# First block's low parts on VectorE alone, weight loads queued ahead of waiting loads, and the places of the last projection's operands

## The chip, the cores and the metric

The kernel runs on one core of a Trainium2 chip. The metric is device microseconds from start to end of one execution. TensorE (PE) does matmuls and PEld its weight loads, VectorE is DVE, ScalarE is ACT, GpSimd is POOL, and SyncE (SP) only issues DMAs.

## The reference

36 tiles of 128 tokens go through three stages, all in float32:

```
attention in chunks of 64:  attn = softmax(q k^T / 8),  out = attn v
first MLP (512 -> 2048 -> 512):   h = x w_in;  g = h * clip(h + 3, 0, 6) / 6;  x' = g w_out
second MLP (512 -> 1024 -> 512):  h = x' w_in2;  s = h * softmax(h);  y = layernorm(s) * g_ln;  out = y w_out2
```

## The kernel before, in words

**Stages.** Tokens are worked in 9 blocks of 512 (b), each of 4 attention units (u) of 128 tokens. While block b goes through the first MLP, the attention of block b+1 is done in between; block 0's four units are done ahead of it (here "the head"). After the ninth block the second MLP runs over 36 tiles of 128 tokens: h2 (L482, 24 matmuls), softmax, layernorm, and the projection out_t (L564, 24 matmuls) three tiles later.

**Two-part operands.** A float32 operand is cut into a high part (a cast by ScalarE into float32r, L73) and a low part (a subtraction, L74), and each product is three matmuls: high·high, high·low, low·high. So x, g, every weight and the normalised tile l have a `_hi` and a `_lo`; `split` makes both, and its last argument says which engine subtracts.

**One step of the first MLP.** For each of 16 slices f of the hidden width, TensorE does 12 matmuls into `hp` (H(f), L272), ScalarE a relu (L278), VectorE the gate (L282), then g is split, and 12 matmuls add into `acc` (O(f), L298). The program order on TensorE is H(f), O(f-1), H(f+1), O(f), so that H(f+1) covers the work on g(f). `hp`, t, g_hi and g_lo have two buffers each. Every fourth step carries an attention unit: `slot` puts in its scores and its product with v (f = 3, 7, 11, 15), exp and norm (f = 0, 4, 8, 12) and transposes (f = 2, 6, 10, 14).

**Weights in block 0.** The inputs' weights arrive as 64-bit words and are turned into float32 in the first block only: `fetch` loads them (SP), `rescale` (L142, ScalarE) scales the high word, `convert` (VectorE) makes the sign (L152) and two word steps (L157), and `split_w` makes the two parts, the low one on GpSimd. In step f the weights wo f and wi f+3 are converted, and g_lo, too, is made by GpSimd in this block. From block 1 on the weights stand in SBUF and VectorE makes g_lo.

**Order.** Each engine runs its instructions strictly in the order in which the code is written. SP too: a load that waits for a buffer holds all loads behind it.

**Places.** Where a tile lies in a partition is fixed when the program is built. In bytes modulo 512, all tiles that the large matmuls read lie at 192 (x_hi, x_lo, wi, wo, g_hi, g_lo) except l_hi and l_lo of the last projection: they stand in pool b3, behind b2's small [P, 1] tiles, at 0 (the first l_hi at byte 173056, while the wi it meets are at 66240 + 4096 f).

Of the kernel before, what the change touches and what calls it, by code (L numbers as in the profile page):

```python
# [8 lines left out]
F32 = mybir.dt.float32  # L9
F32R = mybir.dt.float32r  # L10
# [11 lines left out]
def tile_kernel(  # L22
# [76 lines left out]
    pbd = ap1.tile([P, 2, H, D], F32, name="pbd")  # L99
    q_t, k_t, v_t, p_t, exps, sums, raws, ready = {}, {}, {}, {}, {}, {}, {}, []  # L100

    def att_tile(pool, tag):
        return pool.tile([P, H, D], F32, tag=tag, name=tag)
# [39 lines left out]

    def convert(*keys):

        work = []
# [4 lines left out]
        for key, r, s in work:  # L151
            nc.vector.tensor_single_scalar(  # L152
                out=s, in_=r[:, :, 1], scalar=-(1 << 31), op=ALU.bitwise_and
            )
        for w, op, shift in ((0, ALU.logical_shift_right, 29), (1, ALU.logical_shift_left, 3)):
            for key, r, s in work:
                nc.vector.scalar_tensor_tensor(  # L157
                    out=s, in0=r[:, :, w], scalar=shift, in1=s, op0=op, op1=ALU.bitwise_or
                )
        for (kind, f), r, s in work:  # L160
            w = s.bitcast(F32)
            if kind == "2" and f >= KD * NS:
                nc.vector.tensor_scalar_mul(
                    out=w, in0=w, scalar1=g_sb[:, f - KD * NS : f - KD * NS + 1]
                )
            t = SLOTS[kind](f, F32R)
            (wo if kind == "o" else wi)[f] = t
            ready.append((t[:, 0], t[:, 1], w))

    def split_w(n=2):  # L170
        while ready and n:
            split(*ready.pop(0), nc.gpsimd)
            n -= 1

    def att_psum():
# [32 lines left out]

    def attn_exp_act(u):
        sc, mx = exps.pop(u)  # L210
        p_t[u] = att_tile(ap2, "p")
        sums[u] = ap2.tile([P, H], F32, tag="sm", name="sm")
        for h in range(H):
# [41 lines left out]

    def attn_pv(u, pb, x_hi, x_lo, ps=att_psum):
# [8 lines left out]
        split(x_hi[:, :, o : o + P], x_lo[:, :, o : o + P], xps)  # L265

# [13 lines left out]

    def moe_g(hp, t, eng):
        nc.vector.scalar_tensor_tensor(  # L282
            out=t, in0=t, scalar=6.0, in1=hp, op0=ALU.min, op1=ALU.mult
        )
        g_hi = gp.tile([P, BT], F32R, tag="g_hi", name="g_hi")
        g_lo = gp.tile([P, BT], F32R, tag="g_lo", name="g_lo")
        split(g_hi, g_lo, t, eng)
        return g_hi, g_lo
# [25 lines left out]

    kbs, qps, vs = [kbd], [], []
    for i in range(3):
# [3 lines left out]
    vs = wo_slot(NF - 7, F32).rearrange("p c (h k) -> p c h k", h=H)  # L320

    load_qk(0)
    load_qk(1, qps[0][:, 0], diagonal(kbs[1], nc.gpsimd))
    load_qk(2, qps[1][:, 0], diagonal(kbs[2], nc.vector))
    fetch("i", 0)
    load_qk(3, qps[2][:, 0], diagonal(kbs[3], nc.gpsimd))
    load_v(0)
    load_v(1)
    fetch("i", 1)
    load_v(2, vs[:, 0])  # L330
    load_v(3, vs[:, 1])
    fetch("o", 0)
    fetch("i", 2)
    fetch("o", 1)
    nc.sync.dma_start(out=g_sb, in_=g_ln)
    make_identity(nc, ident)
    diagonal(pbd, nc.gpsimd)
    nc.gpsimd.memset(three, 3.0)
    xs = new_x()
    attn_scores(0)  # L340
    attn_scores(1)
    load_qk(4)
    attn_norm(0, nc.gpsimd)
    attn_scores(2, h_psum, qps[0][:, 1])
    attn_transpose(0, pbd, h_psum)
    rescale("i", 0)
    attn_norm(1)
    attn_scores(3, h_psum, qps[1][:, 1])
    attn_transpose(1, kbs[1])
    attn_norm(2)  # L350
    attn_pv(0, pbd, *xs)
    load_v(4)
    attn_transpose(2, kbs[2], h_psum)
    attn_norm(3)
    convert(("i", 0))
    attn_pv(1, kbs[1], *xs)
    load_v(5)
    rescale("i", 1)
    attn_transpose(3, kbs[3], h_psum)
    split_w(1)  # L360
    attn_pv(2, kbs[2], *xs)
    convert(("i", 1))
    attn_pv(3, kbs[3], *xs)
    rescale("i", 2)
    split_w(1)
    attn_scores_act(4)
    load_qk(5)
    for f in range(2, NF):
        if f < NF - 7:
            fetch("o", f)  # L370
        if f + 1 < NF:
            fetch("i", f + 1)
    for f in range(NF - 7, NF):
        fetch("o", f)
    convert(("i", 2))
    rescale("o", 0)
    rescale("i", 3)
# [25 lines left out]
    def slot(b, f):  # L403
        ph = (f + 1) % 4
        u = (b + 1) * UPB + (f + 1) // 4
        if ph == 0:
            w = u - 1
            if w < NU:
                attn_pv(w, pbd, *xn[w // UPB])
                p_t.pop(w, None)  # L410
                load_v(w + 2)
            start_scores(u)
        elif u < NU:
            first = u < 2 * UPB
            if ph == 1:
                if u in exps:
                    attn_exp_act(u)
                attn_norm(u)
            elif ph == 2 and not first:
                attn_transpose_dve(u, (0, 1))  # L420
            elif ph == 3:
                if first:
                    attn_transpose(u)
                else:
                    attn_transpose_dve(u, (2, 3))

    pend = []
    for b in range(NB):
        first, last = b == 0, b == NB - 1
        if not last:  # L430
            xn[b + 1] = new_x()
        for f in range(NF):
            h = moe_h(f, *xn[b])
            if first:
                split_w(1)
            pend.append((b, f, moe_g(*h, nc.gpsimd if first or last else nc.vector)))
            if f % 4 == 3:
                slot(b, f)
            if first:
                convert(("o", f), ("i", f + 3))  # L440
            if len(pend) > 1:
# [3 lines left out]
            if first:  # L445
                rescale("o", f + 1)
                rescale("i", f + 4)
            split_w(1 if first else 2)
            if last:
# [24 lines left out]
    def h2(t):  # L474
# [3 lines left out]
        for s in range(NS):  # L478
            n = 0
            for kk in range(KD):  # L480
                for a, w in ((x_hi, 0), (x_hi, 1), (x_lo, 0)):
# [12 lines left out]
        mu = b2.tile([P, 1], F32, tag="mu", name="mu")  # L494
        nc.vector.scalar_tensor_tensor(
# [150 lines left out]
```

## Time and profile before

| | |
|---|---|
| median of 3 runs | 1312.58 us (1311.85 to 1313.03) |
| the profiled execution | 1311.98 us, span 1310.0 us, mean granted TensorE clock 0.995 |
| busy share of the span: PE, DVE, ACT, POOL | 98%, 61%, 44%, 23% |
| matmuls | 6368 |
| waits of TensorE that the trace names | 28.5 us |
| moved by DMA | 92.41 MB |

The span runs from the first to the last instruction; some 2 us lie around it. The profile's page cuts the span into 40 slices of 32.75 us, and a digit there is a busy share in tenths. A timeline row is the start and duration in us, then engine, line, operation, out<-in, form and count, and in brackets the idle time ahead of it with what ended it. A chain row is a piece of the chain of work that ended last: start, duration, engine, output, line and the number of instructions merged.

### The profile page before, as it was taken

The numbers are of one execution on the slowest core, as the hardware profiler recorded it, in microseconds if no ns is written. First come the engines' busy times: TensorE is split into PE (matmuls) and PEld (weight loads), VectorE is DVE, ScalarE is ACT, GpSimd is POOL, SyncE is SP. The second block draws the span as 40 slices with busy tenths as digits, with TensorE's granted clock in tenths as the row PEclk, the third lists the DMA queues.
The fourth block names the chain that finished last, engine by engine and source line by source line (L and its number), as shares of the span: only waits on it lengthen the run. The fifth ranks groups of instructions, "written<-read, shape, count | busy, mean of one in ns | idle before, by whom it ended". The sixth has DMA issues, their size and how long they took to land.

```text
span 1310.0 us, 17877 instructions
## 1 busy us (share of the span) xinstructions
PE 1277.4 (98%) x6368; PEld 1041.7 (80%) x6368; DVE 794.0 (61%) x1556; ACT 581.8 (44%) x1106; POOL 298.5 (23%) x562
## 2 busy tenths in 40 slices
PE   6699999999999999999999999999999999999998
PEld 5566788888888888888888888888888888888887
DVE  6788655655655655656555555469766555555542
ACT  4566422222322222222322222445687666666665
POOL 2465200000000000000000000355355444444444
PEclk9899999999999999999999999999999999999999
DMA  7910110110110210200200200444132221222111
GB/s 236 409 62 25 57 49 25 57 49 25 58 47 25 77 29 25 81 25 25 81 25 28 78 25 1 129 129 129 28 94 82 80 81 49 81 81 73 57 49 57
DMA packets 52649, 92.41 MB, mean 71 GB/s; under 512 B 9552, under 2 KB 18768, under 8 KB 52560
## 3 DMA queue, kind: packets, MB, share of 16 engines
q1 hardware_dynamic: 52560, 91.27, 21.8%
q8 instruction: 50, 0.82, 0.2%
q14 instruction: 39, 0.32, 0.1%
HBM read 62.92 MB, written 18.87 MB: 62 GB/s over the span
## 4 chain that ended last, share of the span: by engine, by line
PE 89%; issue 3%; POOL 3%; DVE 2%; DMA 1%; ACT 1%; SPq 1%; POOLq 0%; ACTq 0%; DVEq 0%
PE acc L298 27%; PE hp L272 26%; PE po L564 15%; PE hp L482 15%; PE att L261 2%; PE att L186 2%; POOL g_lo L74 1%; POOL wo L74 1%; DMA wi<-in_moe_w_in 1%; DVE s L157 1%; POOL wi L74 1%; DVE s L152 1%; SPq L112 0%; DVE x_lo L74 0%; DVE t L282 0%
## 5 line engine op out<-in xcount | busy, mean ns | idle before, releaser
L298 PE MATMUL acc<-g_hi,wo 128*128 128x512 f32 x1152 | 295.0, 397 | 16.1 <-ACT wo L73 14.2
L272 PE MATMUL hp<-x_hi,wi 128*128 128x512 f32 x1152 | 285.1, 390 | 0.0
L298 PEld LDWEIGHTS acc<-g_hi,wo 128*128 128x128 f32 x1152 | 213.1, 189 | 73.1 <-ACT wo L73 18.9
L278 ACT ACTIVATE t<-hp,three 128x512 f32<-128x512 f32 x144 | 99.0, 687 | 372.6 <-PE hp L272 372.2
L272 PEld LDWEIGHTS hp<-x_hi,wi 128*128 128x128 f32 x1152 | 215.9, 188 | 44.9 <-ACT wi L142 0.2
L282 DVE SCALAR_TENSOR_TENSOR t<-t,hp 128x512 f32<-128x512 f32 x144 | 99.1, 688 | 234.4 <-ACT t L278 234.4
L74 POOL TENSOR_TENSOR g_lo<-t,g_hi 128x512 fp32r<-128x512 f32 x32 | 45.8, 1431 | 715.1 <-PE acc L298 672.5
L482 PE MATMUL hp<-wi,x_hi 128*128 128x512 f32 x576 | 177.8, 390 | 0.0
L298 PE MATMUL acc<-g_lo,wo 128*128 128x512 f32 x576 | 154.4, 390 | 0.0
L272 PE MATMUL hp<-x_lo,wi 128*128 128x512 f32 x576 | 153.9, 389 | 0.0
L564 PE MATMUL po<-wi,l_hi 128*128 128x512 f32 x576 | 140.2, 396 | 0.0
L251 DVE STREAM_TRANSPOSE pbd<-p 32x128 f32<-32x128 f32 x448 | 135.3, 302 | 5.7
L73 ACT CAST g_hi<-t 128x512 fp32r<-128x512 f32 x144 | 89.3, 620 | 107.9 <-DVE t L282 107.9
L564 PEld LDWEIGHTS po<-wi,l_hi 128*128 128x128 f32 x576 | 108.3, 188 | 25.6
L482 PEld LDWEIGHTS hp<-wi,x_hi 128*128 128x128 f32 x576 | 108.2, 188 | 23.5
L298 PEld LDWEIGHTS acc<-g_lo,wo 128*128 128x128 f32 x576 | 108.6, 189 | 22.9
L74 POOL TENSOR_TENSOR l_lo<-m,l_hi 128x1024 fp32r<-128x1024 f32 x36 | 86.6, 2406 | 174.1 <-ACT l_hi L73 152.0
L272 PEld LDWEIGHTS hp<-x_lo,wi 128*128 128x128 f32 x576 | 108.1, 188 | 22.5
L74 DVE TENSOR_TENSOR g_lo<-t,g_hi 128x512 fp32r<-128x512 f32 x112 | 77.6, 693 | 76.8 <-ACT g_hi L73 76.8
L516 ACT COPY m<-tr 32x256 f32<-32x256 f32 x288 | 115.8, 402 | 2.9
L482 PE MATMUL hp<-wi,x_lo 128*128 128x512 f32 x288 | 112.4, 390 | 0.0
L491 ACT ACTIVATE e<-hp,nmx 128x1024 f32<-128x1024 f32 x36 | 40.2, 1116 | 111.3 <-DVE nmx L488 111.3
(91 smaller groups left out, 1299.7 us busy)
## 6 DMA issues: line engine op xcount, KB each, us to landing
wi<-in_moe_w_in SPq DMA_DIRECT2D x24, 512.0 KB, 7.3
x2d<-xo SPq DMA_DIRECT2D x36, 256.0 KB, 2.8
xo<-x2d SPq DMA_DIRECT2D x36, 256.0 KB, 4.3
m<-tr SPq DMA_DIRECT2D x288, 32.0 KB, 1.8
out<-ob SPq DMA_DIRECT2D x36, 256.0 KB, 2.2
v<-in_v SPq DMA_DIRECT2D x34, 256.0 KB, 2.6
q<-in_q SPq DMA_DIRECT2D x33, 256.0 KB, 3.5
kbd<-in_k SPq DMA_DIRECT2D x66, 128.0 KB, 3.5
```

The costliest lines, as they stand in the source:

```text
L73: nc.scalar.copy(out=hi, in_=src)
L74: (eng or nc.vector).tensor_sub(out=lo, in0=src, in1=hi.bitcast(F32))
L186: nc.tensor.matmul(sc[r0 : r0 + D, h // 2], qt[:, h], kt[:, :, h], start=True, stop=True)
L251: nc.vector.transpose(out=pb[o : o + 32, s // 2, c, s % 2], in_=pv[s * 32 : s * 32 + 32, c, e],)
L272: nc.tensor.matmul(hp, wi[f][:, a, kk * P : (kk + 1) * P], b[:, kk], start=(n == 0), stop=(n == 3 * KD - 1),)
L278: nc.scalar.activation(out=t, in_=hp, func=AF.Relu, bias=three[:])
L282: nc.vector.scalar_tensor_tensor(out=t, in0=t, scalar=6.0, in1=hp, op0=ALU.min, op1=ALU.mult)
L298: nc.tensor.matmul(acc[dc], wo[f][:, w, dc * P : (dc + 1) * P], g[i], start=(f == 0 and n == 0), stop=(f == NF - 1 and n == 2),)
L482: nc.tensor.matmul(hp[:, s * DM : (s + 1) * DM], a[:, kk, o : o + P], wi[kk * NS + s][:, w], start=(n == 0), stop=(n == 3 * KD - 1),)
L491: nc.scalar.activation(out=e, in_=hp, func=AF.Exp, bias=nmx, accum_out=r)
L516: move(out=m[b * 32 : b * 32 + 32, a], in_=tr[a * 32 : a * 32 + 32, b])
L564: nc.tensor.matmul(po, a[:, f], wi[KD * NS + f][:, w], start=(n == 0), stop=(n == 3 * NF2 - 1),)
```

## The change

Low parts of g and of the weights are made by VectorE in block 0, in an order of three steps: in step f the signs of wo f+1 and wi f+3 stand between the gate and g_lo, the word steps behind the subtractions, and what they give is split in the next step (`split_w_hi`, `split_w_lo`, `moe_split` with `between`). An attention unit's exps are cut into two halves over two steps, with the norm moved to f = 1, 5, 9, 13. In the head the scores go to the four `acc` banks, the v products to `h`, the norm of unit 2 to GpSimd, the first weight's conversion stands ahead of norm 3, and low parts of x are put off. Weight loads are queued in ahead of q, k and v loads that wait for a buffer. In the second MLP the small tiles get a pool of their own (`bs`), and l_hi and l_lo three buffers with names of their own, which puts them at 192 modulo 512 (l_hi0 at byte 172736).

The core of the diff:

```diff
+    def split_w_hi(n=1):
         while ready and n:
-            split(*ready.pop(0), nc.gpsimd)
+            hi, lo, w = ready.pop(0)
+            nc.scalar.copy(out=hi, in_=w)
+            halves.append((hi, lo, w))
             n -= 1
+
+    def split_w_lo(eng):
+        for hi, lo, w in halves:
+            eng.tensor_sub(out=lo, in0=w, in1=hi.bitcast(F32))
+        halves.clear()
...
+    def moe_split(t, eng, between=None):
         g_hi = gp.tile([P, BT], F32R, tag="g_hi", name="g_hi")
         g_lo = gp.tile([P, BT], F32R, tag="g_lo", name="g_lo")
-        split(g_hi, g_lo, t, eng)
+        nc.scalar.copy(out=g_hi, in_=t)
+        if between:
+            between()
+        eng.tensor_sub(out=g_lo, in0=t, in1=g_hi.bitcast(F32))
         return g_hi, g_lo
...
     attn_transpose(1, kbs[1])
-    attn_norm(2)
-    attn_pv(0, pbd, *xs)
+    rescale("i", 0)
+    attn_norm(2, nc.gpsimd)
+    attn_pv(0, pbd, *xs, h_psum, lo=False)
     load_v(4)
-    attn_transpose(2, kbs[2], h_psum)
+    fetch("o", 2)
+    fetch("i", 4)
+    convert(("i", 0))
+    attn_transpose(2, kbs[2])
     attn_norm(3)
-    convert(("i", 0))
-    attn_pv(1, kbs[1], *xs)
+    attn_pv(1, kbs[1], *xs, h_psum, lo=False)
     load_v(5)
...
+    ahead = [[("o", f + 1), ("i", f + 3)] for f in range(NF)]
+    ahead[0].insert(0, ("i", 2))
...
-            h = moe_h(f, *xn[b])
+            hp, t = moe_h(f, *xn[b])
+            moe_gate(hp, t)
             if first:
-                split_w(1)
-            pend.append((b, f, moe_g(*h, nc.gpsimd if first or last else nc.vector)))
+
+                split_w(1, nc.vector)
+                g = moe_split(t, nc.vector, lambda: convert_signs(*ahead[f]))
+                split_w_hi(4)
+                split_w_lo(nc.vector)
+                convert_words()
+            else:
+                g = moe_split(t, nc.gpsimd if last else nc.vector)
+            pend.append((b, f, g))
             if f % 4 == 3:
                 slot(b, f)
-            if first:
-                convert(("o", f), ("i", f + 3))
             if len(pend) > 1:
                 moe_o(*pend.pop(0))
...
             if first:
-                rescale("o", f + 1)
+                rescale("o", f + 2)
                 rescale("i", f + 4)
-            split_w(1 if first else 2)
+            else:
+                split_w(2)
...
-    b3 = ctx.enter_context(tc.tile_pool(name="b3", bufs=3, reuse_waits="tile"))
+    b3 = ctx.enter_context(tc.tile_pool(name="b3", bufs=1, reuse_waits="tile"))
+    bs = ctx.enter_context(tc.tile_pool(name="bs", bufs=2, reuse_waits="tile"))
...
+    def l_tile(name, i):
+        return b3.tile([P, NF2, P], F32R, tag=f"{name}{i}", name=f"{name}{i}")
...
-        l_hi = b3.tile([P, NF2, P], F32R, tag="l_hi", name="l_hi")
-        l_lo = b3.tile([P, NF2, P], F32R, tag="l_lo", name="l_lo")
+        l_hi, l_lo = l_tile("l_hi", t % 3), l_tile("l_lo", t % 3)
```

**VectorE, step f = 3 of block 0.** Before, this is the gate of step 3 and what follows up to the next conversions (t is g's first form, s the word being built; wo3 and wi6 are the weights converted):

```order
L282 SCALAR_TENSOR_TENSOR t_568<-t_568,hp_555 128x512
L74 TENSOR_TENSOR x_lo_398<-att_577,x_hi_397 128x4x128
L205 TENSOR_REDUCE mx_599<-att_590 128x8
L206 TENSOR_SCALAR mx_599<-mx_599 128x8
L152 TENSOR_SCALAR s_606<-wo3_340 128x512
L152 TENSOR_SCALAR s_607<-wi6_350 128x512
L157 SCALAR_TENSOR_TENSOR s_606<-wo3_340,s_606 128x512
```

With the change, the same step:

```order
L311 SCALAR_TENSOR_TENSOR t_574<-t_574,hp_561 128x512
L186 TENSOR_TENSOR wo3_538<-s_527,wo3_538 128x512
L151 TENSOR_SCALAR s_582<-wo4_287 128x512
L151 TENSOR_SCALAR s_584<-wi6_289 128x512
L321 TENSOR_TENSOR g_lo_580<-t_574,g_hi_579 128x512
L186 TENSOR_TENSOR wi5_539<-s_529,wi5_539 128x512
L159 SCALAR_TENSOR_TENSOR s_582<-wo4_287,s_582 128x512
L159 SCALAR_TENSOR_TENSOR s_584<-wi6_289,s_584 128x512
L159 SCALAR_TENSOR_TENSOR s_582<-wo4_287,s_582 128x512
L159 SCALAR_TENSOR_TENSOR s_584<-wi6_289,s_584 128x512
L294 TENSOR_TENSOR x_lo_399<-att_595,x_hi_398 128x4x128
L223 TENSOR_REDUCE mx_617<-att_608 128x8
```

Three subtractions (wo3, g_lo, wi5) have come in, and wo is converted a step earlier than before.

**SP, the loads around q and k of unit 4** (q_177 and q_174 are those of unit 4, v_248 and v_278 or v_281 those of v 4 and 5). Before:

```order
L135 DMA wo1_137<-in_moe_w_out 128x1024
L335 DMA g_sb_60<-in_moe_g_ln 128x8
L110 DMA q_177<-in_q 128x512
L112 DMA kbd_93<-in_k 64x512 x2
L120 DMA v_248<-in_v 128x512
L120 DMA v_278<-in_v 128x512
L110 DMA q_332<-in_q 128x512
L112 DMA kbd_93<-in_k 64x512 x2
L135 DMA wo2_336<-in_moe_w_out 128x1024
L135 DMA wi3_338<-in_moe_w_in 128x1024
```

Now:

```order
L110 DMA q_174<-in_q 128x512
L112 DMA kbd_93<-in_k 64x512 x2
L135 DMA wo1_178<-in_moe_w_out 128x1024
L135 DMA wi3_180<-in_moe_w_in 128x1024
L120 DMA v_248<-in_v 128x512
L135 DMA wo2_250<-in_moe_w_out 128x1024
L135 DMA wi4_252<-in_moe_w_in 128x1024
L120 DMA v_281<-in_v 128x512
L135 DMA wo3_283<-in_moe_w_out 128x1024
```

wi3 stood behind the loads of v 4, v 5 and unit 5; now it stands ahead of all three, and wo2 to wi7 ahead of unit 5's.

**ScalarE, the end of the head** (the casts L285 make x_hi of units 1 to 3, L180 a weight's high part, L258 copies transposed probabilities; with the change):

```order
L285 CAST x_hi_144<-hp_271 128x4x128
L258 COPY wo13_99<-att_292 64x512 x2
L180 CAST wi0_258<-s_254 128x512
L142 ACTIVATE wi1_131<-wi1_131 128x512
L285 CAST x_hi_144<-hp_303 128x4x128
L142 ACTIVATE wo0_133<-wo0_133 128x512
L285 CAST x_hi_144<-hp_315 128x4x128
L180 CAST wi1_387<-s_383 128x512
L142 ACTIVATE wi2_135<-wi2_135 128x512
L142 ACTIVATE wo1_178<-wo1_178 128x512
L142 ACTIVATE wi3_180<-wi3_180 128x512
L307 ACTIVATE t_413<-hp_400,three_59 128x512
```

The rescales of wi1 and wo0 now stand ahead of the last two x_hi, and three rescales ahead of the first relu (L307).

## Rows read from the trace of the kernel before

**Rows 1.** The page: busy time by engine, 40 slices of TensorE, one group.

```profile
PE 1277.4 (98%) x6368; PEld 1041.7 (80%) x6368; DVE 794.0 (61%) x1556; ACT 581.8 (44%) x1106; POOL 298.5 (23%) x562
...
PE   6699999999999999999999999999999999999998
...
L74 DVE TENSOR_TENSOR g_lo<-t,g_hi 128x512 fp32r<-128x512 f32 x112 | 77.6, 693 | 76.8 <-ACT g_hi L73 76.8
```

**Rows 2.** Windows: width; busy us of PE, PEld, DVE, ACT, POOL; clock; DMA.

```profile
40.00:50.00 10.00, 6.88 (x21) 5.58 (x22) 9.93 (x15) 5.39 (x14) 4.83 (x4) 0.63 1.03 409
100.00:110.00 10.00, 8.07 (x32) 5.75 (x33) 9.21 (x14) 5.57 (x10) 6.49 (x5) 1.00 0.01 2
160.00:180.00 20.00, 20.00 (x112) 16.48 (x111) 10.94 (x25) 5.73 (x9) 0.00 (x0) 1.00 0.14 40
```

**Rows 3.** TensorE's waits: us in total, times, longest.

```profile
PE acc L298 <- ACT wo L73: 14.2, 7, 9.6
...
PE acc L298 <- POOL wo L74: 1.7, 10, 0.2
```

**Rows 4.** The chain in the first block.

```profile
81.99 1.47 POOL g_lo L74
...
110.49 1.47 POOL g_lo L74
...
138.97 0.44 PE att L236 x4
...
142.14 1.02 PE att L261 x16
143.17 0.87 PE att L186 x16
...
149.71 2.72 PE acc L298 x12
```

**Rows 5.** Timeline of VectorE and GpSimd in one stretch of block 0.

```profile
60.35 0.69 DVE L74 TENSOR_TENSOR x_lo<-att,x_hi 128x512 fp32r<-128x512 f32 x1 [1.17 <-ACT x_hi L73]
...
60.96 0.68 DVE L205 TENSOR_REDUCE mx<-att 128x8 f32<-128x512 f32 x1
...
61.76 0.43 DVE L152 TENSOR_SCALAR s<-wo 128x512 int32<-128x512 int32 x1
...
62.44 0.69 DVE L157 SCALAR_TENSOR_TENSOR s<-wo,s 128x512 int32<-128x512 int32 x1
...
64.24 0.69 DVE L157 SCALAR_TENSOR_TENSOR s<-wi,s 128x512 int32<-128x512 int32 x1
...
66.36 1.29 POOL L74 TENSOR_TENSOR wi<-s,wi 128x512 fp32r<-128x512 f32 x1
66.40 1.54 DVE L152 TENSOR_SCALAR s<-wo 128x512 int32<-128x512 int32 x1
...
71.70 0.16 DVE L226 TENSOR_SCALAR sm<-sm 128x8 f32<-128x8 f32 x1
...
72.14 1.67 DVE L228 TENSOR_TENSOR p<-p,sm 128x512 f32<-128x512 f32 x1
```

**Rows 6.** Timeline of the head and its end.

```profile
22.13 0.69 DVE L228 TENSOR_TENSOR wo<-wo,sm 128x512 f32<-128x512 f32 x1
...
23.19 1.42 DVE L157 SCALAR_TENSOR_TENSOR s<-wi,s 128x512 int32<-128x512 int32 x2
...
26.44 0.58 ACT L73 CAST x_hi<-att 128x512 fp32r<-128x512 f32 x1 [0.44 <-PE att L261]
...
27.81 2.11 PE L272 MATMUL hp<-x_hi,wi 128*128 128x512 f32 x8
...
35.80 0.65 ACT L142 ACTIVATE wi<-wi 128x512 f32<-128x512 f32 x1 [5.99 <-DMA wi<-in_moe_w_in]
```

**Rows 7.** The chain in the second MLP.

```profile
907.82 21.76 PE hp L482 x96
...
957.31 5.47 PE hp L482 x24
962.78 5.60 PE po L564 x24
...
1283.71 22.41 PE po L564 x96
```

More of the change, by code (lines that the diff above doesn't have):

```diff
@@ L99, in tile_kernel @@
     pbd = ap1.tile([P, 2, H, D], F32, name="pbd")
-    q_t, k_t, v_t, p_t, exps, sums, raws, ready = {}, {}, {}, {}, {}, {}, {}, []
+    q_t, k_t, v_t, p_t, exps, sums, raws = {}, {}, {}, {}, {}, {}, {}
     def att_tile(pool, tag):
@@ L142, in rescale, with convert_signs @@
             nc.scalar.activation(out=r, in_=r, func=AF.Copy, scale=2.0**-112)
-    def convert(*keys):
-        work = []
+    work, ready, halves = [], [], []
+    def convert_signs(*keys):
         for key in keys:
@@ L150, in convert, with convert_words @@
                 work.append((key, raws.pop(key).bitcast(I32), s))
[L151 to L154, printed above, removed]
+                nc.vector.tensor_single_scalar(
+                    out=s, in_=work[-1][1][:, :, 1], scalar=-(1 << 31), op=ALU.bitwise_and
+                )
+    def convert_words():
         for w, op, shift in ((0, ALU.logical_shift_right, 29), (1, ALU.logical_shift_left, 3)):
@@ L168, in convert, with split_w @@
             ready.append((t[:, 0], t[:, 1], w))
-    def split_w(n=2):
+        work.clear()
+    def convert(*keys):
+        convert_signs(*keys)
+        convert_words()
+    def split_w_hi(n=1):
         while ready and n:
-            split(*ready.pop(0), nc.gpsimd)
+            hi, lo, w = ready.pop(0)
+            nc.scalar.copy(out=hi, in_=w)
+            halves.append((hi, lo, w))
             n -= 1
+    def split_w_lo(eng):
+        for hi, lo, w in halves:
+            eng.tensor_sub(out=lo, in0=w, in1=hi.bitcast(F32))
+        halves.clear()
+    def split_w(n=2, eng=None):
+        split_w_hi(n)
+        split_w_lo(eng or nc.gpsimd)
     def att_psum():
@@ L207, in attn_scores_act, with attn_exp_act @@
         exps[u] = sc, mx
[L209 to L213, printed above, removed]
+    def attn_exp_act(u, heads):
+        sc, mx = exps[u]
+        if u not in sums:
+            p_t[u] = att_tile(ap2, "p")
+            sums[u] = ap2.tile([P, H], F32, tag="sm", name="sm")
+        for h in heads:
             nc.scalar.activation(
@@ L254, in attn_transpose_dve, with attn_pv @@
                     )
-    def attn_pv(u, pb, x_hi, x_lo, ps=att_psum):
+    def attn_pv(u, pb, x_hi, x_lo, ps=att_psum, lo=True):
         vt = v_t.pop(u)
@@ L264, in attn_pv, with attn_lo @@
         o = (u % UPB) * P
-        split(x_hi[:, :, o : o + P], x_lo[:, :, o : o + P], xps)
+        hi, lo_ = x_hi[:, :, o : o + P], x_lo[:, :, o : o + P]
+        nc.scalar.copy(out=hi, in_=xps)
+        los.append((lo_, xps, hi))
+        if lo:
+            attn_lo()
+    los = []
+    def attn_lo():
+        lo, xps, hi = los.pop(0)
+        nc.vector.tensor_sub(out=lo, in0=xps, in1=hi.bitcast(F32))
     def moe_h(f, x_hi, x_lo):
@@ L279, in moe_h, with moe_gate @@
         return hp, t
-    def moe_g(hp, t, eng):
+    def moe_gate(hp, t):
         nc.vector.scalar_tensor_tensor(
@@ L312, in moe_o @@
                 nc.sync.dma_start(out=x2d[b, :, dc], in_=xo)
-    kbs, qps, vs = [kbd], [], []
+    kbs, qps = [kbd], []
     for i in range(3):
@@ L320, in tile_kernel, with acc_psum, later @@
     vs = wo_slot(NF - 7, F32).rearrange("p c (h k) -> p c h k", h=H)
+    def acc_psum(i):
+        return lambda: ps_acc.tile([P, DM], F32, tag=f"acc{i}", name=f"acc{i}")
+    def later(f):
+        if f < NF:
+            fetch("i", f)
     load_qk(0)
@@ L324, in tile_kernel @@
     load_qk(2, qps[1][:, 0], diagonal(kbs[2], nc.vector))
-    fetch("i", 0)
     load_qk(3, qps[2][:, 0], diagonal(kbs[3], nc.gpsimd))
@@ L328, in tile_kernel @@
     load_v(1)
-    fetch("i", 1)
+    fetch("i", 0)
     load_v(2, vs[:, 0])
     load_v(3, vs[:, 1])
+    fetch("i", 1)
     fetch("o", 0)
     fetch("i", 2)
-    fetch("o", 1)
-    nc.sync.dma_start(out=g_sb, in_=g_ln)
     make_identity(nc, ident)
@@ L339, in tile_kernel @@
     xs = new_x()
-    attn_scores(0)
-    attn_scores(1)
+    attn_scores(0, acc_psum(0))
+    attn_scores(1, acc_psum(1))
     load_qk(4)
+    fetch("o", 1)
+    fetch("i", 3)
     attn_norm(0, nc.gpsimd)
-    attn_scores(2, h_psum, qps[0][:, 1])
-    attn_transpose(0, pbd, h_psum)
-    rescale("i", 0)
-    attn_norm(1)
-    attn_scores(3, h_psum, qps[1][:, 1])
-    attn_transpose(1, kbs[1])
-    attn_norm(2)
-    attn_pv(0, pbd, *xs)
+    attn_scores(2, acc_psum(2), qps[0][:, 1])
+    attn_transpose(0, pbd)
+    attn_norm(1)
+    attn_scores(3, acc_psum(3), qps[1][:, 1])
+    attn_transpose(1, kbs[1])
+    rescale("i", 0)
+    attn_norm(2, nc.gpsimd)
+    attn_pv(0, pbd, *xs, h_psum, lo=False)
     load_v(4)
-    attn_transpose(2, kbs[2], h_psum)
+    fetch("o", 2)
+    fetch("i", 4)
+    convert(("i", 0))
+    attn_transpose(2, kbs[2])
     attn_norm(3)
-    convert(("i", 0))
-    attn_pv(1, kbs[1], *xs)
+    attn_pv(1, kbs[1], *xs, h_psum, lo=False)
     load_v(5)
-    rescale("i", 1)
-    attn_transpose(3, kbs[3], h_psum)
-    split_w(1)
-    attn_pv(2, kbs[2], *xs)
+    fetch("o", 3)
+    fetch("i", 5)
+    fetch("o", 4)
+    fetch("i", 6)
+    attn_lo()
+    attn_transpose(3, kbs[3])
+    attn_lo()
+    split_w(1, nc.vector)
+    rescale("i", 1)
+    attn_pv(2, kbs[2], *xs, h_psum, lo=False)
+    rescale("o", 0)
+    attn_lo()
+    attn_pv(3, kbs[3], *xs, h_psum, lo=False)
+    attn_lo()
+    attn_scores_act(4)
+    for f in range(5, NF):
+        if f == 6:
+            load_qk(5)
+            nc.sync.dma_start(out=g_sb, in_=g_ln)
+        fetch("o", f)
+        later(f + 2)
     convert(("i", 1))
-    attn_pv(3, kbs[3], *xs)
+    split_w_hi()
+    convert_signs(("o", 0))
+    split_w_lo(nc.vector)
+    convert_words()
     rescale("i", 2)
[L365 to L376, printed above, removed]
+    rescale("o", 1)
     rescale("i", 3)
@@ L416, in slot @@
                 if u in exps:
[L417 to L420, printed above, removed]
+                    attn_exp_act(u, range(H // 2))
+                else:
+                    attn_norm(u)
+            elif ph == 2:
+                if u in exps:
+                    attn_exp_act(u, range(H // 2, H))
+                    attn_norm(u)
+                if not first:
+                    attn_transpose_dve(u, (0, 1))
             elif ph == 3:
@@ L432, in tile_kernel @@
         for f in range(NF):
-            h = moe_h(f, *xn[b])
+            hp, t = moe_h(f, *xn[b])
+            moe_gate(hp, t)
             if first:
-                split_w(1)
-            pend.append((b, f, moe_g(*h, nc.gpsimd if first or last else nc.vector)))
+                split_w(1, nc.vector)
+                g = moe_split(t, nc.vector, lambda: convert_signs(*ahead[f]))
+                split_w_hi(4)
+                split_w_lo(nc.vector)
+                convert_words()
+            else:
+                g = moe_split(t, nc.gpsimd if last else nc.vector)
+            pend.append((b, f, g))
             if f % 4 == 3:
                 slot(b, f)
-            if first:
-                convert(("o", f), ("i", f + 3))
             if len(pend) > 1:
@@ L445, in tile_kernel @@
             if first:
-                rescale("o", f + 1)
+                rescale("o", f + 2)
                 rescale("i", f + 4)
-            split_w(1 if first else 2)
+            else:
+                split_w(2)
             if last:
@@ L486, in h2 @@
                     n += 1
-        nmx = b2.tile([P, 1], F32, tag="nmx", name="nmx")
+        nmx = bs.tile([P, 1], F32, tag="nmx", name="nmx")
         nc.vector.tensor_reduce(out=nmx, in_=hp, axis=AX.X, op=ALU.max, negate=True)
         e = b2.tile([P, FF2], F32, tag="e", name="e")
-        r = b2.tile([P, 1], F32, tag="r", name="r")
+        r = bs.tile([P, 1], F32, tag="r", name="r")
         nc.scalar.activation(out=e, in_=hp, func=AF.Exp, bias=nmx, accum_out=r)
@@ L493, in h2 @@
         nc.vector.reciprocal(out=r, in_=r)
-        mu = b2.tile([P, 1], F32, tag="mu", name="mu")
+        mu = bs.tile([P, 1], F32, tag="mu", name="mu")
         nc.vector.scalar_tensor_tensor(
@@ L520, in chain_square @@
         junk = b2.tile([P, FF2], F32, tag="junk", name="junk", bufs=1)
-        va = b2.tile([P, 1], F32, tag="va", name="va")
+        va = bs.tile([P, 1], F32, tag="va", name="va")
         nc.scalar.activation(out=junk, in_=d, func=AF.Square, accum_out=va)
@@ L529, in chain_rstd @@
         )
-        y = b3.tile([P, 1], F32, tag="y", name="y", bufs=4)
+        y = bs.tile([P, 1], F32, tag="y", name="y", bufs=4)
         yi = y.bitcast(I32)
@@ L537, in chain_rstd @@
         )
-        tt = b2.tile([P, 1], F32, tag="tt", name="tt")
+        tt = bs.tile([P, 1], F32, tag="tt", name="tt")
         for _ in range(3):
```

## The prediction

> **What bounds the kernel now.** I read the page first: TensorE is busy 98% of the span, and its 40 slices show where it isn't, in the first three or four [rows 1]. A gain can come from two places only: from TensorE's idle time at the start, or from making its own instructions shorter. The windows say who is busy there: between 100 and 110 us TensorE works 8.07 of 10 us and VectorE 9.21, and GpSimd 6.49; between 160 and 180 us TensorE works all 20 and GpSimd nothing [rows 2]. TensorE's waits add little (14.2 us for a weight's high part, 9.6 of it at one time, and ten waits for GpSimd's wo of 0.2 at most [rows 3]), so the rest is hidden in matmuls that start late and are counted as busy. The chain is clearer: in block 0 it runs through GpSimd's subtractions, and the same one, g_lo, comes at 81.99 and four steps later at 110.49, so four steps take 28.5 us [rows 4]. TensorE's own work in four steps is eight times 2.72 (H or O, 12 matmuls), 1.02 + 0.87 for an attention unit and 0.44 for its transposes, 24.1 us [rows 4]. Block 0 thus loses 4.4 us in four steps.
>
> Why GpSimd and VectorE are slow together is in the timeline [rows 5]. A sign alone takes 0.43 us; beside a GpSimd subtraction of 1.29 us that began 0.04 us before it, it takes 1.54. VectorE's norm (L228), too, takes 1.67 us there.
>
> **VectorE's new step.** From start to start, VectorE needs 0.34 us for a sign (two from 61.76 to 62.44), 0.60 for a word step (three from 62.44 to 64.24), and 0.61 from the x_lo subtraction to the reduce behind it [rows 5]. It now does in a step the gate, three subtractions and four word steps, 8 x 0.60, and two signs, 0.68: 5.48 us. In every four steps come x_lo, reduce and scaling (60.35 to 61.76, 1.41) and a norm (71.70 to 72.14, 0.44, and a multiplication at 0.60, 1.04) [rows 5]. Four steps: 21.92 + 1.41 + 1.04 = 24.4 us. The subtraction with both inputs in SBUF isn't shown back to back on an undisturbed VectorE; its duration of 0.693 [rows 1] is the upper bound for it, 0.60 the lower, and I take 0.60, since x_lo has the same duration and that pitch. GpSimd has nothing left to do in block 0, so nothing slows the signs.
>
> So VectorE (24.4) and TensorE (24.1) come out nearly equal, and waits between them decide. In the new order VectorE should not wait: the casts by ScalarE run beside it (g_hi is cast during wo_lo and the signs, 1.28 us for a cast of about 0.6), and the gate needs H(f), which TensorE does right after O(f-2), most of a step ahead. One tight place is left: the transposes of f = 2, 6, 10, 14 wait for a norm that stands last in VectorE's step before.
>
> **The start.** ScalarE now has the rescales of wi1 and wo0 ahead of the last x_hi, and VectorE the conversion of wi0 (0.42 + 1.42 [rows 6]) ahead of norm 3, while norm 2 goes to GpSimd. Norm 3, at 22.13 before, I put at 23.4; its transposes, copies and v product follow it, and the two rescales come on top: the last x_hi, 26.44 before, starts at 28.4, and H(0), at 27.81 before, at 29.05 [rows 6]. Then I go on by hand with the same prices. VectorE: the reduce and the scaling to 30.5, wi1's sign and words to 32.4, wo0's sign, wi1_lo at 33.1, wo0's words to 35.1; the first relu stands behind three rescales on ScalarE and ends at 35.6; gate 0 is at 35.65. H(1) starts at 33.1, O(0) at 37.0, after g_hi(0). VectorE's step 0 (three signs, six word steps) ends at 42.1 and step 1 (one subtraction more, and a norm: 7.1) at 49.2. The wait for the load of wi3, which ended 5.99 us of ScalarE's idling at 35.80 [rows 6], is gone, because wi3 is issued ahead of the loads that wait for the head. That costs nothing elsewhere: what it passes, v 4, v 5 and unit 5's q and k, is used when a step or more has gone by.
>
> From step 2 at 49.2, eight steps of VectorE lead to step 10 at 98.0. From there the conversions thin out, and TensorE's own work decides: transposes, then H(11) to O(15) with block 1's first H, twelve times 2.72, one more set of transposes and two attention units: 32.6 + 0.9 + 3.8 = 37.3 us. O(15) ends at 135.3. Before, it ended at 149.71 + 2.72 = 152.4 [rows 4]. Gain 17.1 us. Blocks 1 to 8 have TensorE at 20.00 of 20 us [rows 2] and keep their time.
>
> **The second MLP.** Here TensorE never stops, and a projection takes 5.60 us for 24 matmuls where h2 takes 5.47, and 21.76 for the first 96 (5.44 for 24) when no projection lies between [rows 7]. The forms are equal; 96 projections' matmuls in a row at the end, 22.41, are slow without any change of kind [rows 7]. So it is not the switch. What sets l_hi and l_lo apart from all other operands is their place, 0 modulo 512 against 192. If that is the cause, projections go to 5.44, 36 x 0.16 = 5.8, and h2, whose loss of 0.03 comes only beside slow projections, gives 32 x 0.03 = 0.9: gain 6.7 us. No row shows an equal place with an l tile, so the bounds are 0 and 6.7; I take 6.7, since all the other pairs (L272, L298, L482) run at 2.72 for 12. The Trainium skill, page "SBUF — State Buffer", section "SBUF: two separate sides", speaks against it: TensorE has two independent read ports, for the moving operand and for the weights, and it never waits on anyone, so a place would not matter. By that rule the sum would lack the second gain and be 1295.5 in place of 1288.8.
>
> **Sum.** 1311.98 - 17.1 - 6.7 = 1288.2 for an execution like the profiled one, which lies 0.6 below the median shown: 1288.8, so 1289 us. The likeliest case has a range of its own of 1284 to 1293, by the start (H(0) between 27.8 and 30) and a few tenths per step.
>
> **Rivals.**
> - *Places don't matter.* For it: rows show no mechanism, only that one tile differs in more than its place (GpSimd writes l_lo). Against it: l_hi, which ScalarE writes as it writes x_hi, is as slow. Then 1295.5.
> - *VectorE's full pitch is its duration.* With 0.69 for each of eight instructions, a step takes 0.72 more, ten steps 7.2: 1296; with the rival above 1303. Against it: the word steps' pitch [rows 5].
> - *Slower: lock-step.* If TensorE could not run ahead, VectorE's gate would wait in each step for H(f) and the relu, 2.72 + 0.69 = 3.4 us, and a step would take 9.5 in place of 7.1: over 16 steps 38 us, 1344 without a loss of the second gain. It decides from 1.7 us of waiting a step (23.8 us over 14 steps). For it: every engine runs in order, and the relu stands behind two rescales that wait for loads. Against it: two buffers of hp let H(f) start when gate f-2 is done.
> - *The head gets no later and block 0 is TensorE's alone.* From 27.81, 33 times 2.72 and four attention units end at 127: a gain of 25.6 and in all 1280.
>
> **Chances.** Likeliest 0.62; places don't matter 0.17; full pitch 0.09; better than 1284 0.04; lock-step, in part or in full, 0.05; something that eats all of the gain 0.03. From these: faster by over 0.2% 0.92, within 0.2% (2.6 us, about what a measurement tells from no change) 0.03, slower 0.05. The range reaches from TensorE's bound with a little loss, 1283, to the first two rivals and some of their spread, 1300.
>
> **What would show it.** The steps are right if four steps of block 0 take 24 to 25 us between the same instructions, VectorE is busy 9.5 of 10 us there with signs of 0.43 throughout, H(0) starts near 29, and O(15) ends near 135. The second part is right if a projection takes 5.44 in the chain, and h2 too. I am wrong if VectorE has idle time ahead of the gate in every step, if TensorE's clock falls in the gaps ahead of O(0) and H(2) and the loss isn't made up (it stood at 0.63 between 40 and 50 us [rows 2], after the 9.6 us wait), or if projections stay at 5.60.

## The result and the profile after

The changed kernel takes 1289.59 us (median of 4 runs, 1289.22 to 1290.0) where the kernel before takes 1312.8 beside it (1311.85 to 1313.52): a ratio of 0.9824, 95% interval 0.9807 to 0.9841. The prediction was 1289 us, range 1283 to 1300. The profiled span is 1287.4 us, 22.6 less than before.

The page of the changed kernel, its first lines (busy time by engine, then TensorE's 40 slices):

```profile
PE 1265.1 (98%) x6368; PEld 1041.7 (81%) x6368; DVE 793.8 (62%) x1603; ACT 581.1 (45%) x1106; POOL 235.2 (18%) x515
...
PE   5999999999999999999999999999999999999998
```

The share of busy time is 98% as in [rows 1], though 22.6 us are gone. GpSimd has 63 us less to do and VectorE no more than before: about as much as it took over it had lost before in instructions drawn out beside GpSimd (VectorE's signs took 30.4 us in the first 140 us and take 13.5 now). What changed shows in single stretches. The windows of the changed kernel (columns as in [rows 2]):

```profile
40.00:50.00 10.00, 8.98 (x33) 6.93 (x34) 9.93 (x21) 7.05 (x19) 0.00 (x0) 0.83 1.03 406
100.00:110.00 10.00, 10.00 (x68) 8.18 (x67) 9.96 (x19) 6.44 (x12) 0.00 (x0) 1.00 0.25 80
160.00:180.00 20.00, 20.00 (x112) 16.45 (x111) 12.64 (x30) 5.04 (x8) 0.00 (x0) 1.00 0.13 39
```

Between 100 and 110 us TensorE now works 10.00 of 10 where it worked 8.07. It starts 68 matmuls where it started 32 [rows 2], but 32 of the 68 are the short ones of an attention unit, which fell outside this window before; of the large ones it starts 36 in place of 32. VectorE works 9.96 and GpSimd nothing. The granted clock, 0.63 between 40 and 50 before, is 0.83: a mean over the window of TensorE's two levels, 1.2 and 2.4 GHz.

The chain of the changed kernel, in block 0, at its end and in the second MLP (start, duration, engine, output, line, instructions):

```profile
73.03 0.44 PE att L255 x4
...
97.37 0.44 PE att L255 x4
...
132.47 2.72 PE acc L332 x12
135.19 2.73 PE hp L301 x12
...
891.53 21.76 PE hp L549 x96
913.29 5.44 PE po L633 x24
918.73 5.44 PE hp L549 x24
...
1261.45 21.77 PE po L633 x96
```

The transposes of an attention unit come every 24.3 us, where g_lo came every 28.5 before [rows 4]. O(15) ends at 135.19 in place of 152.43 [rows 4]: 17.24 us. The first transposes of block 0 (f = 2), in the timelines of the kernel before and of the changed one, say where these were gained:

```profile
54.04 0.60 PE L236 MATMUL att<-ident,p 128*128 128x128 f32 x4
```

```profile
48.52 0.60 PE L255 MATMUL att<-ident,p 128*128 128x128 f32 x4
```

They come 5.5 us earlier, which is the gain of the head and the first steps; the twelve steps from there to the last transposes give the other 11.7.

A projection takes 5.44 in place of 5.60 and h2 5.44 in place of 5.47, the last 96 matmuls 21.77 in place of 22.41 [rows 7]; from the first h2 to the end of the last projection it is 391.69 us in place of 398.30 [rows 7], 6.6 less. From O(15)'s end to the second MLP it takes 756.34 in place of 755.39, 0.95 more, and what follows the last matmul is 0.3 longer. -17.24 - 6.61 + 0.95 + 0.3 = -22.6, the difference of the spans.

VectorE in one step of block 0, in the timeline of the changed kernel, from one gate to the next, and the gate four steps after the first (L311 is the gate, L186 the low part of a weight, L321 that of g):

```profile
84.78 0.68 DVE L311 SCALAR_TENSOR_TENSOR t<-t,hp 128x512 f32<-128x512 f32 x1
85.38 0.69 DVE L186 TENSOR_TENSOR wo<-s,wo 128x512 fp32r<-128x512 f32 x1
85.98 0.42 DVE L151 TENSOR_SCALAR s<-wo 128x512 int32<-128x512 int32 x1
86.31 0.42 DVE L151 TENSOR_SCALAR s<-wi 128x512 int32<-128x512 int32 x1
86.65 0.68 DVE L321 TENSOR_TENSOR g_lo<-t,g_hi 128x512 fp32r<-128x512 f32 x1
...
90.26 0.68 DVE L311 SCALAR_TENSOR_TENSOR t<-t,hp 128x512 f32<-128x512 f32 x1
...
109.16 0.68 DVE L311 SCALAR_TENSOR_TENSOR t<-t,hp 128x512 f32<-128x512 f32 x1
```

From 84.78 to 90.26 is 5.48 us, the step as it was added up, and four steps, to 109.16, take 24.38. The subtraction of two operands in SBUF, whose pitch no row of before showed, follows at 0.60 (85.38 to 85.98). The signs take 0.42, no longer 1.54 [rows 5], and no instruction has a wait beside it.

### The profile page after: what moved, and what is told of

Its sections match the earlier page's. It is cut to its first block, busy times and chain, and to the rows that moved or that the text cites. A ratio compares the mean times of both kernels' runs of the same rounds, so it can differ in the third digit from the quotient of the medians.

```text
span 1287.4 us, 17808 instructions
## 1 busy us (share of the span) xinstructions
PE 1265.1 (98%) x6368; PEld 1041.7 (81%) x6368; DVE 793.8 (62%) x1603; ACT 581.1 (45%) x1106; POOL 235.2 (18%) x515
## 4 chain that ended last, share of the span: by engine, by line
PE 94%; DVE 3%; ACT 1%; issue 1%; DMA 0%; SPq 0%; ACTq 0%; DVEq 0%
PE acc L332 30%; PE hp L301 29%; PE po L633 15%; PE hp L549 15%; PE att L280 3%; PE att L204 2%; DVE s L159 1%; DVE t L311 0%; DVE pbd L270 0%; DMA wo<-in_k 0%; DVE s L151 0%; DVE x_lo L74 0%; ACT wi L142 0%; PE att L255 0%; PE acc L204 0%
## 5 line engine op out<-in xcount | busy, mean ns | idle before, releaser
L332 PE MATMUL acc<-g_hi,wo 128*128 128x512 f32 x1152 | 289.4, 393 | 0.7 <-ACT g_hi L318 0.6
L307 ACT ACTIVATE t<-hp,three 128x512 f32<-128x512 f32 x144 | 99.2, 689 | 388.2 <-PE hp L301 388.2
L311 DVE SCALAR_TENSOR_TENSOR t<-t,hp 128x512 f32<-128x512 f32 x144 | 99.2, 689 | 222.0 <-ACT t L307 221.9
L321 POOL TENSOR_TENSOR g_lo<-t,g_hi 128x512 fp32r<-128x512 f32 x16 | 23.3, 1459 | 827.2 <-ACT g_hi L318 827.2
L633 PE MATMUL po<-wi,l_hi 128*128 128x512 f32 x576 | 136.4, 389 | 0.0
L321 DVE TENSOR_TENSOR g_lo<-t,g_hi 128x512 fp32r<-128x512 f32 x128 | 88.6, 692 | 76.9 <-ACT g_hi L318 76.8
```

The source lines that it names most:

```text
L307: nc.scalar.activation(out=t, in_=hp, func=AF.Relu, bias=three[:])
L311: nc.vector.scalar_tensor_tensor(out=t, in0=t, scalar=6.0, in1=hp, op0=ALU.min, op1=ALU.mult)
L321: eng.tensor_sub(out=g_lo, in0=t, in1=g_hi.bitcast(F32))
L332: nc.tensor.matmul(acc[dc], wo[f][:, w, dc * P : (dc + 1) * P], g[i], start=(f == 0 and n == 0), stop=(f == NF - 1 and n == 2),)
L633: nc.tensor.matmul(po, a[:, f], wi[KD * NS + f][:, w], start=(n == 0), stop=(n == 3 * NF2 - 1),)
```

## The experiments

The kernels before beside which these ran had medians of 1312.29 (the first four), 1311.88 (the next four) and 1312.38 (the last).

**The places undone.** In the changed kernel the old pools come back:

```diff
-    b3 = ctx.enter_context(tc.tile_pool(name="b3", bufs=1, reuse_waits="tile"))
-    bs = ctx.enter_context(tc.tile_pool(name="bs", bufs=2, reuse_waits="tile"))
+    b3 = ctx.enter_context(tc.tile_pool(name="b3", bufs=3, reuse_waits="tile"))
...
-        l_hi, l_lo = l_tile("l_hi", t % 3), l_tile("l_lo", t % 3)
+        l_hi = b3.tile([P, NF2, P], F32R, tag="l_hi", name="l_hi")
+        l_lo = b3.tile([P, NF2, P], F32R, tag="l_lo", name="l_lo")
```

> The changed kernel with the second MLP's small tiles and l tiles in their old pools (l at 0 modulo 512 again, everything else unchanged). If the place makes the projections slow: 24 projection matmuls take 5.60 us again and h2 5.47, 6.6 us more than the changed kernel, about 1296.2. If the second MLP became faster for another reason (block 0's engine, the order): 5.44 stays and the time is 1289.6.

Measured: 1296.41 us, ratio to before 0.9882 (0.9867 to 0.9897), 6.8 more than the changed kernel. In its chain the slow projections are back:

```profile
913.98 5.60 PE po L630 x24
919.58 5.47 PE hp L548 x24
```

**The places alone.** The kernel before with the new pools and the l buffers of their own, the same edit the other way round.

> The kernel before with only the pools of the second MLP changed. By the place: 6.6 us less than before, about 1306.2, with the first 900 us as before. By the rival: 1312.8.

Measured: 1305.27 us, ratio 0.9951 (0.9936 to 0.9966), 7.0 less than the 1312.29 beside it; the chain has 5.44 for both, here its first projection:

```profile
929.15 5.44 PE po L567 x24
```

So the second gain is there with or without the rest.

**The order alone.** The changed kernel, its new head and its new queue of loads included, but the three subtractions of a step on GpSimd, as before:

```diff
-                split_w(1, nc.vector)
-                g = moe_split(t, nc.vector, lambda: convert_signs(*ahead[f]))
+                split_w(1, nc.gpsimd)
+                g = moe_split(t, nc.gpsimd, lambda: convert_signs(*ahead[f]))
                 split_w_hi(4)
-                split_w_lo(nc.vector)
+                split_w_lo(nc.gpsimd)
```

> The changed kernel with block 0's three subtractions a step (two weights and g) given back to GpSimd, in the new order. My theory (the gain is that GpSimd no longer slows VectorE and is out of the chain): four steps of block 0 go from 24.3 back to 27 to 29 us, signs of over 1 us appear again, 1301 to 1309. Rival (the new order is what counts, either engine would do): within 3 us of the changed kernel, up to 1293.

Measured: 1307.67 us, ratio 0.9962 (0.995 to 0.9974). The second gain of 6.6 is in it; its O(15) ends at 154.11, 1.7 later than before. The execution profiled is the slowest of its six runs, which reach from 1305.17 to 1308.38 us; what spreads them is not shown. Its timeline, where a sign and a word step meet a subtraction by GpSimd:

```profile
69.32 1.78 DVE L159 SCALAR_TENSOR_TENSOR s<-wi,s 128x512 int32<-128x512 int32 x1
70.51 1.74 POOL L186 TENSOR_TENSOR wi<-s,wi 128x512 fp32r<-128x512 f32 x1
...
74.85 1.47 POOL L321 TENSOR_TENSOR g_lo<-t,g_hi 128x512 fp32r<-128x512 f32 x1
75.09 1.51 DVE L151 TENSOR_SCALAR s<-wi 128x512 int32<-128x512 int32 x1
...
82.26 0.63 PE L255 MATMUL att<-ident,p 128*128 128x128 f32 x4 [3.81 <-DVE p L247]
...
112.20 1.09 PE L255 MATMUL att<-ident,p 128*128 128x128 f32 x4 [3.81 <-DVE p L247]
```

The sign that meets GpSimd's g_lo ends 0.28 us after it, which is little less than its own time: it stood, as far as these rows can tell, until GpSimd was done. VectorE is busy 10.00 of 10 between 100 and 110 us, and four steps, from transposes to transposes, take 29.9 (82.26 to 112.20) and 28.2. The transposes wait 3.81 us for VectorE's norm: VectorE sets the pace, and not TensorE's clock, though that falls in stretches (0.83 between 80 and 90 us). The Trainium skill, page "SBUF — State Buffer", section "Who interferes with whom", says that GpSimd and VectorE, in VectorE's two-port modes or with two of its inputs in SBUF, share one pair of ports as an exclusive lock, and that the one that comes second stands still and isn't merely slowed. For the sign the trace agrees that it stood; a sign has one input, and no run here shows in which mode it ran.

**The engine alone.** The kernel before, in its old order, with VectorE subtracting in block 0:

```diff
-                split_w(1)
-            pend.append((b, f, moe_g(*h, nc.gpsimd if first or last else nc.vector)))
+                split_w(1, nc.vector)
+            pend.append((b, f, moe_g(*h, nc.gpsimd if last else nc.vector)))
...
-            split_w(1 if first else 2)
+            split_w(1 if first else 2, nc.vector if first else None)
```

> The kernel before with block 0's three subtractions on VectorE, everything else in its old order. My theory: VectorE's own work is 24.4 us in four steps here too, but it now waits in order for ScalarE's casts, which stand directly ahead of the subtractions, some 0.6 to 1.2 us a step: 26 to 29 us in four steps, 1303 to 1311. Rival (the engine is all): 24.4 us, and with the old start and old places about 1299.

Measured: 1317.41 us, ratio 1.0041 (1.0025 to 1.0058): slower than before, and above what was expected. GpSimd does nothing there and the signs take 0.42, but four steps take 29.8 us, of the same 24.4 us of work; in the chain:

```profile
61.60 0.69 DVE g_lo L74
...
91.39 0.69 DVE g_lo L74
```

The timeline shows what stands between:

```profile
96.71 2.12 PE L298 MATMUL acc<-g_hi,wo 128*128 128x512 f32 x8 [1.73 <-ACT wo L73]
97.79 0.69 DVE L74 TENSOR_TENSOR wi<-s,wi 128x512 fp32r<-128x512 f32 x1 [0.41 <-ACT wi L73]
98.40 0.68 DVE L282 SCALAR_TENSOR_TENSOR t<-t,hp 128x512 f32<-128x512 f32 x1
99.11 0.62 ACT L73 CAST g_hi<-t 128x512 fp32r<-128x512 f32 x1 [1.35 <-DVE t L282]
99.76 0.69 DVE L74 TENSOR_TENSOR g_lo<-t,g_hi 128x512 fp32r<-128x512 f32 x1 [0.69 <-ACT g_hi L73]
```

In the old order each subtraction stands right behind the cast it needs. From the gate at 98.40 to g_lo at 99.76 pass 1.36 us in place of 0.60, and from wo's subtraction at 96.69 to wi's at 97.79 1.10 in place of 0.60; ahead of wo's subtraction stand 0.2 more. With 0.76 in each of the four steps from 61.60 on, and 0.7 to 0.8 in three of them for the casts of the weights, that is the 5.4 us by which four steps are too long. In the changed kernel a subtraction of the step before and two signs fill the place between gate and g_lo (the timeline above). The engine alone costs 4.4 us by spans; the order alone gains nothing in block 0 that shows above the 3 us by which its runs spread (in the one profiled, block 0 ends 1.7 later); the two together gain 17.2. What the new head is worth by itself no run shows.

**The loads as before.** The changed kernel with the weight loads in SP's old order.

```diff
     load_qk(4)
-    fetch("o", 1)
-    fetch("i", 3)
...
     load_v(4)
-    fetch("o", 2)
-    fetch("i", 4)
...
+    load_qk(5)
+    for f in range(2, NF):
```

> The changed kernel with SP's loads in their old order (the first wi early, later weights behind the loads of v 4, v 5 and unit 5). My theory: wi3 lands near 35 us again, its rescale stands ahead of the first relu on ScalarE, so the first gate comes some 2 us later and so does all up to the last transposes: 2 to 4 us more, 1291.5 to 1293.5. Rival (hidden, since VectorE is the bound at the start): within 0.5 us of the changed kernel, 1289.6.

Measured: 1291.75 us, ratio 0.9848 (0.9835 to 0.9862); its span is 2.7 longer, and its O(15) ends 2.8 later. The waits in its timeline, at ScalarE's third rescale and behind it:

```profile
36.18 0.67 ACT L142 ACTIVATE wi<-wi 128x512 f32<-128x512 f32 x1 [1.47 <-DMA wi<-in_moe_w_in]
...
38.85 2.14 PE L332 MATMUL acc<-g_hi,wo 128*128 128x512 f32 x8 [2.23 <-ACT g_hi L318]
```

wi3's load holds the rescale for 1.47 us, the first relu stands behind it, and O(0) waits 2.23 where the changed kernel waits 0.61.

That is about half of the 2.8 us. The other half is lost before wi3 is waited for: H(0) comes at 29.59 here and at 28.20 in the changed kernel, 1.39 later. In the head TensorE stands 2.71 us ahead of unit 0's transposes (1.64 in the changed kernel), and the granted clock falls to 0.54 between 14.5 and 17 us, near the lower of its two levels, 1.2 GHz, where the changed kernel has 1.00. Unit 3's scores then take 1.98 us in place of 1.09, first with the old order of loads, then in the changed kernel:

```profile
14.97 1.98 PE L204 MATMUL acc<-wo,wo 128*64 128x128 f32 x16
```

```profile
14.44 1.09 PE L204 MATMUL acc<-wo,wo 128*64 128x128 f32 x16
```

What was expected named wi3's load alone. So the queue is worth 2 to 3 us, all of it at the start, and its parts are some 1.4 us each.

**The start eased.** From H(0) on, the waits of TensorE that remain in the changed kernel are few: 0.9 for x_hi ahead of H(0), 1.0 and 1.7 for a weight's high part ahead of H(1) and H(2), 0.5 for a weight's low part within H(2), 0.6 for g_hi ahead of O(0), and 0.5 for unit 8's transposed probabilities. This kernel does wi1's rescale and conversion while VectorE and ScalarE idle in the head, puts wo0's rescale behind the last x_hi, and leaves the exps and the norm of unit 8 whole and in their old step:

```diff
+    rescale("i", 1)
     attn_lo()
     attn_transpose(3, kbs[3])
     attn_lo()
-    split_w(1, nc.vector)
-    rescale("i", 1)
+    split_w_hi()
+    convert(("i", 1))
+    split_w_lo(nc.vector)
     attn_pv(2, kbs[2], *xs, h_psum, lo=False)
-    rescale("o", 0)
...
-                    attn_exp_act(u, range(H // 2))
-                else:
+                    attn_exp_act(u, range(H // 2 if first else H))
+                if not (first and u in exps):
                     attn_norm(u)
```

> The changed kernel with wi1's rescale and conversion moved forward into VectorE's idle time of the head, wo0's rescale behind the last x_hi, and unit 8's exps and norm undivided again. If VectorE's continuous work from 28 us on sets when TensorE is saturated: that comes 1.5 to 2 us earlier, and block 1's wait for unit 8 of 0.5 us and what goes with it, 0.9 in all, goes: 2.4 to 2.9 us less than the changed kernel, about 1287. If only TensorE's two waits of 1 us counted: 0.9 to 1.5 us less, 1288.4.

Measured: 1285.1 us (1284.61 to 1287.36, 5 runs), ratio 0.9802 (0.9788 to 0.9815): faster than both kernels. The span is 4.3 us below the changed kernel's, more than was expected. H(0), gate 0 and the end of block 0 in its timeline and its chain:

```profile
27.36 2.08 PE L301 MATMUL hp<-x_hi,wi 128*128 128x512 f32 x8 [0.33 <-ACT wi L180]
...
31.19 0.69 DVE L311 SCALAR_TENSOR_TENSOR t<-t,hp 128x512 f32<-128x512 f32 x1 [0.30 <-ACT t L307]
...
129.18 2.72 PE acc L332 x12
```

O(15) ends at 131.90, 3.3 earlier. H(0) comes only 0.84 earlier, but VectorE has wi1's conversion behind it by then: gate 0 is at 31.19 in place of 34.46, and this 3.27 stays to the end of the block: in both kernels VectorE has next to no idle time from gate 0 on until the conversions thin out. From O(15) to the second MLP it takes 755.33 us again, so the 0.95 that block 1 had lost came from unit 8's exps and norm, the only part of the edit that reaches past block 0.

**Which places are equal.** Two kernels give the three l buffers, which the tiles use in turn, a place each (tile 0's, 1's, 2's), by padding ahead of them; in bytes modulo 512 beyond the equal place: 64, 128 and 256 in the first, 32, 320 (the place before the change) and 0 in the second.

```diff
+    PADS = {'l_hi0': 64, 'l_hi1': 64, 'l_hi2': 128}
+
     def l_tile(name, i):
-        return b3.tile([P, NF2, P], F32R, tag=f"{name}{i}", name=f"{name}{i}")
+        key = f"{name}{i}"
+        if PADS.get(key):
+            b3.tile([P, PADS[key] // 4], F32, tag=f"pad{key}", name=f"pad{key}")
+            del PADS[key]
+        return b3.tile([P, NF2, P], F32R, tag=key, name=key)
```

> The changed kernel with pads between the l tiles, so that the three buffers (tile number modulo 3) stand 64, 128 and 256 bytes further modulo 512 than the operands they meet. If an equal place modulo 512 is needed: every projection takes about 5.6 us. If modulo 256 is enough, only tiles 2, 5, 8 and so on take 5.44; if 128, those and tiles 1, 4, 7; if 64, all of them. If what is bad is the place 0 alone: all 5.44.

> The same with the three buffers 32, 320 (the place of before, 0 modulo 512) and 0 bytes further modulo 512, the last at another multiple of 512 than in the changed kernel. If equal places modulo 512 are the rule: tiles 2, 5, 8 take 5.44 us, tiles 1, 4, 7 take 5.60, tiles 0, 3, 6 more than 5.44. If larger multiples count too: no tile is at 5.44.

Measured: 1294.76 and 1294.32 us, one run each. The first three projections in the chain of the first:

```profile
914.65 5.60 PE po L639 x24
...
925.73 5.59 PE po L639 x24
...
936.77 5.44 PE po L639 x24
```

And of the second:

```profile
914.17 5.59 PE po L639 x24
...
925.21 5.60 PE po L639 x24
...
936.27 5.44 PE po L639 x24
```

The next three repeat them in both. So 256 beyond is as good as equal, and 32, 64, 128 and 320 are equally slow: there is no degree in it.

**All at another place.** To tell "equal places" from "0 is a bad place", everything is moved by 320 bytes, so that all operands stand at 0:

```diff
+    const.tile([P, 80], F32, name="pad")
```

> The changed kernel with 320 bytes of padding behind its constants, so that all operands of the large matmuls, l_hi and l_lo among them, stand at 0 modulo 512 bytes in place of 192. Two readings of the slow projections are left. If what counts is that the two operands of a matmul stand at equal places, nothing changes: a projection stays at 5.44 us for 24 matmuls, and so do h2's and the 12 of H and O at 2.72; the span stays within 1 us of the 1287.4 of the changed kernel. If the place 0 itself were slow for a moving or a stationary operand, all large matmuls would go to 5.6 per 24 (2.8 per 12), and the time would grow by some 3%, about 35 us.

Measured: 1289.77 us in one run, span 1288.0; projections and h2 at 5.44:

```profile
913.87 5.44 PE po L634 x24
919.31 5.44 PE hp L550 x24
```

It is the difference of the two places that counts, not the place.

## Why the prediction was right

**VectorE's step.** The 5.48 us came out to the hundredth, and four steps of VectorE take 24.38 where 24.4 was added up. TensorE's own four steps take 24.34, without a gap in the chain (73.03 to 97.37), where the prediction had 24.1: it had counted the O behind an attention unit at 2.72, and that takes 2.94. So the two engines are as nearly equal as was said, both are full from 50 us until the conversions thin out, and there a shorter step of VectorE alone would have gained next to nothing. Of the two bounds for the subtraction's pitch, 0.60 holds, which settles the rival of full pitch. VectorE has no wait ahead of its gate in that stretch, so there is no lock-step. What was argued for the order (that the casts run beside VectorE's other work) is what the engine alone shows by its lack; there I had expected a smaller loss, because I counted fewer of the casts as uncovered. The time expected there did not follow from its own steps either: 29 us in four steps, its upper end, is more than the 28.5 of before, and so cannot go with 1311.

**The start.** Here the sum was off by about a microsecond, and was right by luck. Norm 3 was put at 23.4 and came at 22.55, since wi0's conversion began early, in idle time of VectorE; H(0) came at 28.20 (29.05 forecast), gate 0 at 34.46 (35.65), step 1 ended at 48.02 (49.2). That 1.2 us was taken back in two places: the transposes come half a microsecond behind the gate from which I counted them, and an O behind an attention unit takes 2.94, not 2.72, two times in the last stretch. O(15) ended at 135.19 against 135.3.

The timeline of the changed kernel at norm 3, H(0), gate 0 and H(2):

```profile
22.55 0.69 DVE L247 TENSOR_TENSOR wo<-wo,sm 128x512 f32<-128x512 f32 x1
...
28.20 2.11 PE L301 MATMUL hp<-x_hi,wi 128*128 128x512 f32 x8 [0.94 <-ACT x_hi L285]
...
34.46 0.69 DVE L311 SCALAR_TENSOR_TENSOR t<-t,hp 128x512 f32<-128x512 f32 x1 [0.25 <-ACT t L307]
...
40.53 1.21 PE L301 MATMUL hp<-x_hi,wi 128*128 128x512 f32 x4 [1.67 <-ACT wi L180]
```

**The clock.** The granted clock did fall, to 0.83 between 40 and 50 us, after such gaps as the 1.67 ahead of H(2) in the last row. The last 8 matmuls of H(2) take 3.49 us in the chain, where eight at 2.72 for 12 would take 1.81. Little of that reaches the end: VectorE is busy 9.93 of 10 there, and the transposes of f = 2, at 48.52, need a norm that VectorE ends at 48.10, so without the fall they could have come some 0.4 us earlier at most (an estimate from these two times).

**Blocks 1 to 8.** "Keep their time" was wrong by 0.95 us: I had looked at TensorE's 20.00 of 20 and not at the norm of unit 8, which the change moved a step later in block 1 as well. The matmuls with v wait 0.53 us for its transposes, and the eased start, where the norm is back, has no such loss:

```profile
149.68 0.98 PE L280 MATMUL att<-pbd,v 128*64 128x128 f32 x13 [0.53 <-DVE pbd L270]
```

**The second MLP.** 6.61 us against 6.7. The rival by which places do not matter is out: undoing the places alone gives all of it back, and making them alone gives all of it. The step from "equal modulo 512" is right in effect and too narrow as a rule: modulo 256 is enough.

## What to carry to other kernels

Where two engines slow each other, moving the work to one of them is half the change: the kernel with only the engine changed was slower, because its order left the wait for ScalarE's casts, which GpSimd had stood through before, to VectorE. Put work that is ready, from the step before or the step after, between a producer's cast and the subtraction that needs it. And when the same form of matmul shows two durations, compare the places of its two operands before looking for a wait: none was shown here, and 36 projections held 5.8 us, besides the 0.9 that h2 lost next to them.

## What was not expected of the hardware

That a matmul's time depends on the places of its operands in a partition: 24 matmuls of 512 columns take 5.44 us when both operands start at equal places modulo 256 bytes and 5.59 to 5.60 when they don't, which is 227 against 233 ns each, with no wait in the trace. Tried were differences of 0 and 256 (fast) and 32, 64, 128 and 320 (slow), all with float32r operands in this kernel. The Trainium skill, page "SBUF — State Buffer", section "SBUF: two separate sides", says, as cited in the prediction, that TensorE never waits on anyone, and by that there would have been no difference; the runs show one, and they decide. The places are those that the build gave the tiles; no trace shows an address. What in the chip causes the difference stays open: that the reads of the moving operand and of the weights meet somewhere would fit, but no run here shows it.
